# One store and one load a tile in a fused attention and gated MLP block, y and the result on GpSimd's queue, and the first half of w_in loaded early

## The chip, the cores and the metric

The kernel runs on one core of a Trainium2 chip. A core has five engines with an instruction stream each: TensorE (PE in the profile, with its weight loads as PEld), VectorE (DVE), ScalarE (ACT), GpSimd (POOL) and SyncE (SP), which only issues transfers. A transfer (DMA) is issued by an instruction on one of these streams, waits there for what it needs, and is then carried by the core's 16 DMA engines; "SPq", "ACTq" and "POOLq" are the issuing streams. The metric is the device time of the program in microseconds (us), lower is better; the time before is the median of three runs.

## The reference

One transformer block on x of 2048 tokens (S) by 640 (D), all in float32:

```python
h  = x + A_ref(layernorm(x), wqkv, wo)
h2 = h + B_ref(layernorm(h), w_in, w_sp, b_sp, w_out)
```

`A_ref` is attention with 32 heads of 20 values, causal, over a window of 256 tokens, followed by the projection with `wo`. `B_ref` is a gated MLP that mixes tokens:

```python
z = gelu(x @ w_in)                      # 2048 x 1728
z1, z2 = z[..., :864], layernorm(z[..., 864:])
g = w_sp @ z2 + b_sp[:, None]           # over tokens, 2048 x 2048
out = (z1 * g) @ w_out
```

## The kernel before

Tokens are cut into 16 tiles of 128. Every float32 product on TensorE is made of three products of a high and a low part (hi x hi, hi x lo, lo x hi), so each operand is first split: ScalarE or VectorE rounds the high part, VectorE subtracts it from the raw value for the low part. The two large products of the MLP use a scheme of seven block products instead of eight, whose block sums VectorE, ScalarE or GpSimd form beforehand.

The stages, in order of time. First layernorm, v, q and k. Then attention in 128 steps (`for s in range(NU + 2)`, L662), in which SP's order is the order in which the code is written; the sums of the softmax go through DRAM (`o_d`, then `r_d`, read back as `rs`). Then for each tile i `wo_tile(i)` (L1354): it scales o by the reciprocal sums (`norm_o`, L168), splits it (`split_o`, L173 to L177), multiplies it with wo (`proj_o`, L98), adds x (`load_x2` brings it, L144), and makes the layernorm of the result, `hn(i)`, in one of six buffers `hb`. `store_hn(i)` (L853) writes hn to DRAM. `z_pair` (L879) reads the rows of hn back with `load` (L896), turns them with a 32x32 block transpose on VectorE (L859), splits them and makes the first half of z (z1) with the first half of w_in; the blocks of that half are prepared by `win1_prep` (L779), a generator of which `wo_tile` takes three pieces a tile. `z2_pair` does the second half, `first_gate` and `second_gate` the products with w_sp, each over half of the tokens. In `second_gate(p)` (L1265) the gate is added up in `rows`, multiplied with z1 into y (`gated`, L1282), and y of two tiles is stored (`store_y`, L1210), loaded back with its blocks moved (`load_y`, L1215), turned (`turn_y`, L1220) and split (`split_y`, L139 and L140). `final` (L1244) multiplies it with w_out two pairs later, adds h (`load_h`, L1242) and stores the result (L1261). The last four tiles run behind the last step (L1412).

Both round trips through DRAM (hn, y) exist because VectorE transposes only within 32x32 blocks: the trip moves the blocks to other partitions. Before, hn's store is cut in four, one for each group of 32 tokens, and writes rows whose parts are already in block order; y's store is one transfer and its load is four:

```python
for a in range(4):
    nc.sync.dma_start(dst[a], hn(i)[32 * a:32 * a + 32].rearrange("j (b c) -> j b c", b=4))
```

Behind attention (`ms.close()`, L701) the order on each engine is not the order of the code: a planner orders every instruction by the code's order and by its own estimate of when its inputs are there. A `dict` named `later` (`at(n, f)`, L870) gives the step before which a piece of work is written. An engine executes its stream in order: an instruction that waits holds up all behind it.

w_in's first half has 5 row blocks of 128 x 864. Blocks 0 and 2 are loaded at step 126 of attention (L224) into `wraw`, blocks 1 and 3 into two of the `rows` buffers behind the third piece of `win1_prep` (L791), block 4 into `wraw` again behind the seventh (L793).

Of the kernel before, what the change touches and what calls it, by code (L numbers as in the profile page):

```python
# [15 lines left out]
P = 128  # L16
# [19 lines left out]
def block_kernel(ctx, tc, x, wqk, wv, wo, w_in, wsp, bsp, w_out, out):  # L36
# [19 lines left out]
    hn_d = dram.tile([NT, P, D], F32, name="hn_d")  # L56
# [49 lines left out]
    def open_early(pl):  # L106
        mem["m1"] = pl.tile([P, 6 * D + 6 * P], F32, name="m1")
        mem["xh"] = [pl.tile([P, D], F32, name=f"xh{i}") for i in range(4)]
        mem["inv"] = [pl.tile([P, P], F32, name=f"inv{i}") for i in range(2)]
        mem["wraw"] = pl.tile([P, 2, 2, HF], F32, name="wraw")  # L110
# [82 lines left out]
    def load_win1(b):  # L193
        nc.sync.dma_start(mem["wraw"][:, b], w_in[2 * b * P:(2 * b + 1) * P, :FH].rearrange("k (h c) -> k h c", h=2))

    def proj_early(s):
# [24 lines left out]
        if s == 125:  # L221
            split_o(1, True)
        if s == 126:
            for b in range(2):  # L224
                load_win1(b)
            tiles, mem["rs"], _ = load_o(2)
            tiles()
        if s == 127:
            for i in (2, 3):
                load_x2(i)  # L230
# [548 lines left out]
    def win1_prep(raw):  # L779
        seven, last = win1  # L780
        rest = [r.rearrange("p (h c) -> p h c", h=2) for r in rows[2:]]

# [4 lines left out]
        for n, f in enumerate(pieces(0, [raw[:, b] for b in range(2)], 1.0)):  # L787
            f()
            if n == 2:
                for b in range(2):  # L790
                    nc.sync.dma_start(rows[2 + b], w_in[(2 * b + 1) * P:(2 * b + 2) * P, :FH])  # L791
            yield
        nc.sync.dma_start(raw[:, 0], w_in[4 * P:, :FH].rearrange("k (h c) -> k h c", h=2))  # L793
        yield
        yield
        for f in pieces(1, rest, ones[:, 0:1]):
            f()
            yield
        yield
        for j in range(2):  # L800
            hi, lo = two(last[j])
            nc.scalar.activation(hi, raw[:, 0, j], AF.Copy, scale=ones[:, 1:2])
            minus(lo, raw[:, 0, j], hi.bitcast(F32))
        yield
# [13 lines left out]
    mem["xh"].append(ep.tile([P, D], F32, name="xh4"))  # L818
    mem["hb"] = [ep.tile([P, D], F32, name=f"hb{i}") for i in range(6)]
# [33 lines left out]
    def store_hn(i):  # L853
        dst = hn_d[i].rearrange("(b j) (a c) -> a j b c", b=4, a=4)
        for a in range(4):
            nc.sync.dma_start(dst[a], hn(i)[32 * a:32 * a + 32].rearrange("j (b c) -> j b c", b=4))
# [22 lines left out]
    def z_pair(q, i, j, w):  # L879
# [16 lines left out]
        def load():  # L896
            nc.sync.dma_start(ri, hn_d[i])
            nc.sync.dma_start(rj, hn_d[j])
# [550 lines left out]
```

## Time and profile before

| | |
|---|---|
| median of three runs | 1097.06 us (1095.64 to 1097.12) |
| the profiled execution's own time | 1099.3 us |
| its span, first to last instruction | 1097.6 us |
| mean granted clock of TensorE | 0.993 |
| HBM read and written | 129.00 MB and 72.86 MB |

The profile is of one execution. A row of a timeline gives start and length in us, engine, line, operation, output and inputs, and how often; in brackets stands the idle time of the engine before it and what ended it. A row of a source view gives min/median/max in ns, first and last start. A busy TensorE is not TensorE at its peak, but an idle one is lost time as long as nothing later absorbs it.

### The profile page before, as it was taken

To read this page: it belongs to the slowest core of one execution; us is meant where nothing else is said; L and a number is where in the kernel's file an instruction comes from. 1 tells how busy PE (TensorE), PEld (TensorE's weight loads), DVE (VectorE), ACT (ScalarE), POOL (GpSimd) and SP (SyncE) were. 2 spreads that over 40 slices of the span, in tenths; PEclk is the share of its full clock that TensorE was granted. 3 is DMA by queue.
4 is the path that set the end of the run, shared out by engine and by line. 5 is a ranking of instruction groups with operands and counts; after the bars stand their busy time and mean duration, and the time that the engine had idled before them with its cause. 6 is when DMAs were issued, how large, how long until landed. Compare 5 with 4: busy or idle time off the path is not lost.

```text
span 1097.6 us, 27487 instructions
## 1 busy us (share of the span) xinstructions
PE 1068.1 (97%) x10475; PEld 959.0 (87%) x10475; DVE 750.4 (68%) x2059; ACT 559.3 (51%) x1164; POOL 367.9 (34%) x526
## 2 busy tenths in 40 slices
PE   8999999999999999998999999999999999999998
PEld 7998877668888787698999999899999989989998
DVE  6541222879999999768867687767737895766553
ACT  4333443239999999747755567433426531222110
POOL 3114444457777777701000065265332000000000
PEclk9999999999999999999999999999999999999999
DMA  7212565565666664589855521456493587877554
GB/s 264 73 36 89 162 221 183 180 222 182 206 209 209 200 204 122 155 286 273 277 183 164 200 88 39 136 183 222 175 334 141 183 261 195 247 209 212 166 158 131
DMA packets 113077, 202.47 MB, mean 184 GB/s; under 512 B 13696, under 2 KB 74768, under 8 KB 109024
## 3 DMA queue, kind: packets, MB, share of 16 engines
q1 hardware_dynamic: 108304, 186.77, 53.8%
q0 software_dynamic: 2336, 8.70, 2.2%
q10 hardware_dynamic: 2304, 5.24, 1.3%
q8 instruction: 82, 1.34, 0.5%
q14 instruction: 51, 0.42, 0.1%
HBM read 129.00 MB, written 72.86 MB: 184 GB/s over the span
## 4 chain that ended last, share of the span: by engine, by line
PE 64%; DVE 11%; DMA 10%; issue 4%; POOL 4%; ACT 4%; SPq 2%; POOLq 0%; DVEq 0%; ACTq 0%
PE bank_a L1177 17%; PE bank_b L1235 6%; PE pv L437 6%; PE bank L343 5%; PE bank L409 5%; PE bank_a L929 4%; PE bank_b L929 3%; PE wo_ps L98 2%; PE qk L527 2%; PE qk L528 2%; PE qk L529 2%; DVE row L724 2%; ACT pt L412 2%; DVE zl L724 2%; PE bank_a L982 1%
## 5 line engine op out<-in xcount | busy, mean ns | idle before, releaser
L412 ACT ACTIVATE pt<-bank 128x384 f32<-128x384 f32 (+2 forms) x512 | 200.9, 497 | 10.5 <-PE bank L409 6.5
L1177 PE MATMUL bank_a<-zl,aw 128*128 128x432 f32 x759 | 168.1, 358 | 0.0
L355 DVE CUSTOM_DVE_ANT_0 junk<-bank,strip 128x288 bf16<-128x288 f32 x392 | 157.8, 454 | 3.3 <-PE bank L343 1.7
L730 ACT ACTIVATE aw<-fx 128x512 fp32r<-128x512 f32 (+3 forms) x147 | 85.1, 592 | 135.9 <-PE bank_a L1177 65.2
L1177 PEld LDWEIGHTS bank_a<-zl,aw 128*128 128x128 f32 x759 | 142.6, 188 | 6.0
L1177 PE MATMUL bank_a<-ze,aw 128*128 128x432 f32 x573 | 132.5, 359 | 4.1 <-DVE row L724 1.8
L437 PE MATMUL pv<-pt,v_sb 128*32 128x192 f32 (+3 forms) x1984 | 126.2, 322 | 2.9 <-POOL pt L414 1.1
L1177 PEld LDWEIGHTS bank_a<-ze,aw 128*128 128x128 f32 x573 | 106.1, 188 | 11.2 <-DVE row L724 2.9
L724 DVE TENSOR_TENSOR aw<-fx,aw 128x512 fp32r<-128x512 f32 (+3 forms) x146 | 100.1, 697 | 13.1 <-ACT aw L730 12.2
L409 PE MATMUL bank<-slot 123*32 123x288 bf16 (+5 forms) x1536 | 106.0, 280 | 1.6 <-ACT pt L412 0.7
L414 POOL TENSOR_SCALAR_AFFINE_SELECT pt<-pt 128x512 f32<-128x512 f32 x128 | 82.9, 648 | 44.5 <-ACT pt L412 43.4
L724 DVE TENSOR_TENSOR row<-bank_a,row 128x432 f32<-128x432 f32 x95 | 56.9, 602 | 58.0 <-PE bank_a L1177 40.9
L1235 PE MATMUL bank_b<-wout,y_sp 128*128 128x320 f32 (+1 forms) x588 | 92.1, 313 | 3.0 <-DVE y_sp L140 2.0
L982 PE MATMUL bank_a<-win,aw 128*128 128x432 f32 x480 | 95.0, 359 | 0.0
L982 PEld LDWEIGHTS bank_a<-win,aw 128*128 128x128 f32 x480 | 90.4, 188 | 3.8
L1235 PEld LDWEIGHTS bank_b<-wout,y_sp 128*128 128x128 f32 (+1 forms) x588 | 89.6, 191 | 4.1 <-DVE y_sp L140 2.4
L343 PE MATMUL bank<-slot 120*32 120x288 bf16 (+2 forms) x1264 | 89.1, 283 | 1.5 <-DVE mcol L355 1.0
L543 DVE TENSOR_TENSOR rest<-qk,sg 128x512 f32<-128x512 f32 x40 | 27.7, 692 | 86.9 <-ACT sg L541 86.9
L417 POOL TENSOR_SCALAR_AFFINE_SELECT pt<-pt 128x512 f32<-128x512 f32 x112 | 74.5, 665 | 0.0
L546 POOL TENSOR_TENSOR sg<-rest,sg 128x512 bf16<-128x512 f32 x40 | 46.6, 1166 | 70.1 <-ACT sg L545 65.8
L409 PEld LDWEIGHTS <-slot 123*32 123x32 bf16 x1536 | 52.6, 96 | 16.7 <-issue 5.7
L437 PEld LDWEIGHTS pv<-pt,v_sb 128*32 128x32 f32 x1984 | 59.1, 110 | 8.5 <-POOL pt L417 3.0
(198 smaller groups left out, 2178.6 us busy)
## 6 DMA issues: line engine op xcount, KB each, us to landing
fx<-wsp_in SPq DMA_DIRECT2D x30, 512.0 KB
slot<-qk_d SPq DMA_DIRECT2D x72, 200.0 KB
qk_d<-sg SPq DMA_DIRECT2D x32, 384.0 KB
slot<-qk_d SPq DMA_DIRECT2D x72, 160.0 KB
fx<-hn_d SPq DMA_DIRECT2D x32, 320.0 KB
o_d<-ot SPq DMA_DIRECT2D x64, 128.0 KB
z_d<-row SPq DMA_DIRECT2D x18, 432.0 KB
y_d<-z SPq DMA_DIRECT2D x16, 448.0 KB
```

The costliest lines, as they stand in the source:

```text
L343: nc.tensor.matmul(ps[32 * j:32 * j + 32, :n], part(st, half, 120, 0, hh, q0, 32), part(st, half, 120, 1, hh, lo + skip * j, n), start=Tru ...
L355: nc.vector.tensor_tensor_reduce(out=junk[:, :n], in0=ps[:, :n], in1=keep, scale=1.0, scalar=NEG, op0=OP.add, op1=OP.max, accum_out=m_cols ...
L409: nc.tensor.matmul(ps[32 * i:32 * i + 32, b:e], part(st, half, 123, 1, hh, k0, 32), part(st, half, 123, 0, hh, kb * P + b, e - b), start=T ...
L412: nc.scalar.activation(pt[:, hh, :n], ps[:, :n], AF.Exp, scale=SCALE)
L414: nc.gpsimd.affine_select(out=pt[:, :, :P], in_=pt[:, :, :P], pattern=[[0, 4], [1, P]], base=0, channel_multiplier=-1, compare_op=OP.is_ge ...
L437: nc.tensor.matmul(ps[32 * hh:32 * hh + 32, a - 512 * c:b - 512 * c], v_sb[:, kb, v0:v0 + 32], pt[:, hh, a - kb * P:b - kb * P], start=fir ...
L724: (eng or nc.vector).tensor_tensor(out=out, in0=a, in1=b, op=op)
L730: nc.scalar.activation(out, a, AF.Copy)
L929: nc.tensor.matmul(ps, a[x], b[:, y], start=start and m + x + y == 0, stop=stop and m == n - 1 and x == 1, skip_group_check=True)
L982: nc.tensor.matmul(b[0][:, :HF], a[t][:, x, kk], win2[0][:, y, kk, h * HF:(h + 1) * HF], start=kk + x + y == 0, stop=kk == KD - 1 and x == 1)
L1177: nc.tensor.matmul(ps, w[m][x][:, k], zc[k][m][:, y], start=start and k + x + y == 0, stop=stop and k == 3 and x == 1, skip_group_check=True)
L1235: nc.tensor.matmul(ps[j][:, :HD], y[:w, a, k, :], e1["wout"][:w, b, k, j * HD:(j + 1) * HD], start=(k == 0 and a + b == 0), stop=(k == KF ...
```

## The change

hn is stored in one transfer, as four planes of 160 columns (`hn_d` is now `[NT, 4, P, D // 4]`), and read back with four consecutive tokens in one row of 640 (`hn_rows`). The tokens of a tile therefore come out of the transpose in another order: position 32a + j holds token 4j + a. z, z1, z2 and g keep that order, and w_sp and b_sp are permuted to it on the host. y's load takes the same form, in one transfer, and orders the tokens once more; h is loaded and the result is stored through a view (`twice_turned`) that has the same order on the DRAM side.

y's stores and loads and the result's stores of the first 12 of 16 tiles are issued on GpSimd (`queue(n)`); those of the last four stay on SP. h's loads stay on SP.

All five blocks of w_in's first half have a tile of their own in `wraw` and are loaded at attention's steps 114 to 122, one at every second step. `wo_tile` takes three pieces of `win1_prep` for the first two tiles and two for the others. The fifth buffer of x (`xh`) is opened with the others, the load of x's tile 4 moves to step 127, and hn has five buffers in place of six.

```diff
-    hn_d = dram.tile([NT, P, D], F32, name="hn_d")
+    hn_d = dram.tile([NT, 4, P, D // 4], F32, name="hn_d")
...
-        mem["wraw"] = pl.tile([P, 2, 2, HF], F32, name="wraw")
+        mem["wraw"] = [pl.tile([P, 2, HF], F32, name=f"wraw{i}") for i in range(KD)]
...
-        nc.sync.dma_start(mem["wraw"][:, b], w_in[2 * b * P:(2 * b + 1) * P, :FH].rearrange("k (h c) -> k h c", h=2))
+        nc.sync.dma_start(mem["wraw"][b], w_in[b * P:(b + 1) * P, :FH].rearrange("k (h c) -> k h c", h=2))
...
+        if 114 <= s < 124 and s % 2 == 0:
+            load_win1((0, 2, 1, 3, 4)[(s - 114) // 2])
         if s == 126:
-            for b in range(2):
-                load_win1(b)
             tiles, mem["rs"], _ = load_o(2)
             tiles()
         if s == 127:
-            for i in (2, 3):
+            for i in (2, 3, 4):
                 load_x2(i)
             mem["rs"]()
...
-        for n, f in enumerate(pieces(0, [raw[:, b] for b in range(2)], 1.0)):
-            f()
-            if n == 2:
-                for b in range(2):
-                    nc.sync.dma_start(rows[2 + b], w_in[(2 * b + 1) * P:(2 * b + 2) * P, :FH])
-            yield
-        nc.sync.dma_start(raw[:, 0], w_in[4 * P:, :FH].rearrange("k (h c) -> k h c", h=2))
-        yield
-        yield
-        for f in pieces(1, rest, ones[:, 0:1]):
-            f()
-            yield
-        yield
+        for k in range(2):
+            for f in pieces(k, [raw[k], raw[k + 2]], ones[:, 0:1] if k else 1.0):
+                f()
+                yield
...
-    mem["hb"] = [ep.tile([P, D], F32, name=f"hb{i}") for i in range(6)]
+    mem["hb"] = [ep.tile([P, D], F32, name=f"hb{i}") for i in range(5)]
...
     def store_hn(i):
-        dst = hn_d[i].rearrange("(b j) (a c) -> a j b c", b=4, a=4)
-        for a in range(4):
-            nc.sync.dma_start(dst[a], hn(i)[32 * a:32 * a + 32].rearrange("j (b c) -> j b c", b=4))
+        nc.sync.dma_start(hn_d[i].rearrange("b p c -> p b c"), hn(i).rearrange("p (b c) -> p b c", b=4))
+
+    def hn_rows(i):
+        return hn_d[i].rearrange("b (j a) c -> (b j) (a c)", a=4)
...
+    def queue(n):
+        return nc.gpsimd if n < NT - 4 else nc.sync
+
     def store_y(n):
-        nc.sync.dma_start(y_d[n].rearrange("b p c -> p b c"),
+        queue(n).dma_start(y_d[n].rearrange("b p c -> p b c"),
                           e1["z1"][n % 2].rearrange("p (b c) -> p b c", b=4))

     def load_y(n):
-        for b in range(4):
-            nc.sync.dma_start(e1["yt"][n % 2][32 * b:32 * b + 32].rearrange("j (a c) -> j a c", a=4),
-                              y_d[n, b].rearrange("(a j) c -> j a c", a=4))
+        queue(n).dma_start(e1["yt"][n % 2], y_d[n].rearrange("b (j a) c -> (b j) (a c)", a=4))
...
+    def twice_turned(d):
+        return d.rearrange("(b a) c -> a b c", a=16)
+
     def load_h(n):
-        nc.sync.dma_start(e1["h"][n % 2], h_d[tile_of(n)])
+        nc.sync.dma_start(e1["h"][n % 2], twice_turned(h_d[tile_of(n)]))
...
-            nc.sync.dma_start(out[tile_of(n) * P:(tile_of(n) + 1) * P, c], ht[:, c])
+            queue(n).dma_start(twice_turned(out[tile_of(n) * P:(tile_of(n) + 1) * P, c]), ht[:, c])
...
-        for n in (4,) if i == 0 else (i + 4,) if i + 4 < NT else ():
-            load_x2(n)
+        if 0 < i < NT - 4:
+            load_x2(i + 4)
...
-        for _ in range(3):
+        for _ in range(3 if i < 2 else 2):
             next(w1, None)
...
-    wsp = np.asarray(B_w_sp).reshape(NT, P, NT, P).transpose(0, 3, 2, 1)
-    bsp = np.asarray(B_b_sp).reshape(NT, P).T
+    order = np.arange(P).reshape(32, 4).T.reshape(P)
+    wsp = np.asarray(B_w_sp).reshape(NT, P, NT, P)[:, order][..., order].transpose(0, 3, 2, 1)
+    bsp = np.asarray(B_b_sp).reshape(NT, P)[:, order].T
```

More of the change, by code (lines that the diff above doesn't have):

```diff
@@ L107, in open_early @@
         mem["m1"] = pl.tile([P, 6 * D + 6 * P], F32, name="m1")
-        mem["xh"] = [pl.tile([P, D], F32, name=f"xh{i}") for i in range(4)]
+        mem["xh"] = [pl.tile([P, D], F32, name=f"xh{i}") for i in range(5)]
         mem["inv"] = [pl.tile([P, P], F32, name=f"inv{i}") for i in range(2)]
-        mem["wraw"] = pl.tile([P, 2, 2, HF], F32, name="wraw")
+        mem["wraw"] = [pl.tile([P, 2, HF], F32, name=f"wraw{i}") for i in range(KD)]
     def view(flat, lo, *shape):
@@ L780, in win1_prep @@
         seven, last = win1
-        rest = [r.rearrange("p (h c) -> p h c", h=2) for r in rows[2:]]
         def pieces(k, blocks, one):
@@ L786, in win1_prep @@
         yield
-        for n, f in enumerate(pieces(0, [raw[:, b] for b in range(2)], 1.0)):
-            f()
-            if n == 2:
-                for b in range(2):
-                    nc.sync.dma_start(rows[2 + b], w_in[(2 * b + 1) * P:(2 * b + 2) * P, :FH])
-            yield
-        nc.sync.dma_start(raw[:, 0], w_in[4 * P:, :FH].rearrange("k (h c) -> k h c", h=2))
-        yield
-        yield
-        for f in pieces(1, rest, ones[:, 0:1]):
-            f()
-            yield
-        yield
+        for k in range(2):
+            for f in pieces(k, [raw[k], raw[k + 2]], ones[:, 0:1] if k else 1.0):
+                f()
+                yield
         for j in range(2):
             hi, lo = two(last[j])
-            nc.scalar.activation(hi, raw[:, 0, j], AF.Copy, scale=ones[:, 1:2])
-            minus(lo, raw[:, 0, j], hi.bitcast(F32))
-        yield
+            nc.scalar.activation(hi, raw[4][:, j], AF.Copy, scale=ones[:, 1:2])
+            minus(lo, raw[4][:, j], hi.bitcast(F32))
+            yield
     def win2_prep(raw):
@@ L817, in block_kernel @@
     ep = pool(early_stack, "early2")
-    mem["xh"].append(ep.tile([P, D], F32, name="xh4"))
-    mem["hb"] = [ep.tile([P, D], F32, name=f"hb{i}") for i in range(6)]
+    mem["hb"] = [ep.tile([P, D], F32, name=f"hb{i}") for i in range(5)]
     zc_stack, win_stack = (ctx.enter_context(ExitStack()) for _ in range(2))
@@ L896, in load @@
         def load():
-            nc.sync.dma_start(ri, hn_d[i])
-            nc.sync.dma_start(rj, hn_d[j])
+            nc.sync.dma_start(ri, hn_rows(i))
+            nc.sync.dma_start(rj, hn_rows(j))
         a11, a12, a21, a22 = (turned(r, k, k + 2) for r in (ri, rj) for k in (0, 2))
@@ L990, in z2_pair @@
             soon = q == 13
-            at(m - (5 if soon else 12 if q == 8 else 6), lambda t=t, tile_t=tile_t: nc.sync.dma_start(r[t], hn_d[tile_t]))
+            at(m - (5 if soon else 12 if q == 8 else 6), lambda t=t, tile_t=tile_t: nc.sync.dma_start(r[t], hn_rows(tile_t)))
             at(m - (1 if soon else 3), lambda t=t: prep(t, True, None))
```

## The prediction

> **What bounds the kernel now.** I read the page first, then the table of stages, then TensorE's timeline wherever a stage shows it idle, and then the queue (SP) and VectorE (DVE) at those places.
>
> ```profile
> span 1097.6 us, 27487 instructions
> PE 1068.1 (97%) x10475; PEld 959.0 (87%) x10475; DVE 750.4 (68%) x2059; ACT 559.3 (51%) x1164; POOL 367.9 (34%) x526
> ```
>
> TensorE (PE) is idle for 1097.6 - 1068.1 = 29.5 us of the span. Only idle time of PE, and time in which its clock is lowered, can be won by a change that touches transfers alone. The stages show where that is; the columns are stage, length, busy us of PE, weight load, DVE, ACT, POOL, granted clock, DMA share and GB/s.
>
> ```profile
> 428.00:440.00 12.00, 11.11 (x289) 8.23 (x285) 10.52 (x32) 11.47 (x34) 10.21 (x18) 1.00 0.35 105
> 440.00:465.00 25.00, 22.48 (x431) 15.20 (x424) 17.67 (x22) 18.80 (x52) 18.96 (x25) 1.00 0.48 143
> 465.00:525.00 60.00, 54.02 (x322) 52.30 (x323) 47.91 (x115) 35.30 (x66) 6.61 (x8) 0.91 0.89 280
> 525.00:630.00 105.00, 105.00 (x581) 101.74 (x580) 75.49 (x165) 65.31 (x118) 6.80 (x9) 1.00 0.64 204
> 880.00:970.00 90.00, 85.53 (x485) 81.94 (x486) 63.72 (x104) 21.00 (x32) 0.00 (x0) 1.00 0.81 238
> 970.00:1071.00 101.00, 101.00 (x585) 98.74 (x584) 61.18 (x96) 19.03 (x26) 0.00 (x0) 0.98 0.61 176
> ```
>
> The change works in two stages with losses. In 465 to 525 (attention over, first output projections and z products) PE idles 5.98 us, its clock is 0.91, and the DMA engines are 89% busy. In 880 to 970 (start of the second gates) it idles 4.47 us. From 525 to 630, where most of hn's stores lie, and from 970 to 1071, PE is never idle: there the change can win nothing.
>
> **The gaps of 465 to 525 on PE** (in brackets the idle time before the row, and what ended it):
>
> ```profile
> 480.94 0.85 PE L98 MATMUL wo_ps<-xb,xb 128*128 128x320 f32 x4 [2.02 <-DVE xb L177]
> 514.10 1.01 PE L929 MATMUL bank_b<-zl,aw 128*128 128x432 f32 x3 [1.24 <-ACT tmp L730]
> 517.83 1.45 PE L929 MATMUL bank_b<-zl,aw 128*128 128x432 f32 x3 [2.72 <-DVE aw L724]
> ```
>
> The same stretch in tens of microseconds (columns as above):
>
> ```profile
> 480.00:490.00 10.00, 9.06 (x51) 9.06 (x52) 8.01 (x19) 5.39 (x10) 0.85 (x1) 0.83 0.88 287
> 490.00:500.00 10.00, 10.00 (x70) 10.00 (x69) 9.31 (x24) 6.11 (x11) 2.64 (x3) 1.00 0.93 307
> 500.00:510.00 10.00, 10.00 (x67) 9.91 (x66) 10.00 (x24) 6.87 (x15) 0.66 (x1) 1.00 0.95 282
> 510.00:520.00 10.00, 6.04 (x25) 4.94 (x24) 7.01 (x18) 7.30 (x14) 1.91 (x2) 0.81 0.86 254
> 520.00:530.00 10.00, 10.00 (x53) 9.64 (x53) 8.08 (x22) 6.98 (x13) 0.55 (x1) 0.85 0.88 274
> ```
>
> The gaps are 2.02 + 1.24 + 2.72 = 5.98 us. A clock of 0.83, 0.81 and 0.85 over 10 us costs 1.7, 1.9 and 1.5 us; at half clock that is 3.4 us behind the first gap, and 3.8 + 3.0 us around the last two. If the second spell is unbroken it began at 516.2, so that 1.6 us of it lie inside the gap that ends at 517.83 and cost nothing more (0.8 us taken off): 1.7 + 2.6 = 4.3 us. The stage loses 5.98 + 4.3 = 10.3 us.
>
> The Trainium skill (TensorE: Matmul & The Clock Gate, section "Part 1: The HAM clock gate (the "warmup" mystery)") has the clock halve after an idle window of about 3.4 us; by that rule a gap of 2.02 us would cost nothing more and the stage could give back 5.98 us only. The trace disagrees: 0.83 behind a gap of 2.02 us.
>
> **What is late there.** The queue before the first gap, and before the last:
>
> ```profile
> 445.47 3.17 SPq L152 DMA_DIRECT2D m<-o_d  x5
> 462.58 1.06 SPq L194 DMA_DIRECT2D wraw<-w_in_in  x2
> 463.68 4.46 SPq L152 DMA_DIRECT2D m<-o_d  x5
> 468.24 0.58 SPq L392 DMA_DIRECT2D r_d<-inv  x1
> 471.38 0.52 SPq L158 DMA_DIRECT2D m<-r_d  x1
> 474.97 1.56 DVE L168 TENSOR_TENSOR m<-m 128x640 f32<-128x640 f32 x2 [4.57 <-DMA m<-r_d]
> 498.00 1.77 SPq L856 DMA_DIRECT2D hn_d<-hb  x4
> 500.35 2.48 SPq L856 DMA_DIRECT2D hn_d<-hb  x4
> 503.40 2.57 SPq L856 DMA_DIRECT2D hn_d<-hb  x4
> 509.48 0.60 SPq L158 DMA_DIRECT2D m<-r_d  x1
> 514.75 1.56 DVE L168 TENSOR_TENSOR m<-m 128x640 f32<-128x640 f32 x2 [2.99 <-DMA m<-r_d]
> ```
>
> DVE waits twice for reciprocal row sums (m<-r_d). The store that they are read back from goes out at 468.24 only after two loads of w_in and five slow ones of o_d; the later load goes out at 509.48 after three groups of hn stores. Everything behind these waits on DVE, the split that PE needs included (L177, L724), comes late.
>
> **The change, part by part.** *hn's store as one issue.* The layout in DRAM still has runs of 160 values (640 B), so packets and bytes stay; 64 issues become 16. Their price is that of y's store, also one issue of 128 x 4 runs:
>
> ```profile
> L856 SPq DMA_DIRECT2D hn_d<-hb x64: 302/432/1056, 476.9 to 586.1; - x64
> L1210 SPq DMA_DIRECT2D y_d<-z x16: 370/377/434, 875.8 to 1072.7; - x16
> ```
>
> The queue wins 64 x 0.432 - 16 x 0.377 = 21.6 us, but on the path only the three groups count: 1.77 + 2.48 + 2.57 - 3 x 0.377 = 5.7 us, against a DVE wait of 2.99. The read side keeps whole rows; the new token order costs nothing on the chip, since w_sp and b_sp are permuted on the host and h and the result keep one run a row in the DRAM side's new order.
>
> *w_in's five loads moved* to steps 114 to 122 of 128, that is to about 428 to 446 (an estimate: step 126 issued its two loads at 462.58, and a step takes some 2 to 3 us). They pass attention's stores and o_d's first loads on the queue (five issues, some 0.5 us each, where the queue is not full). 5 x 432 KB at 280 GB/s is 7.9 us of transfers that leave the stage behind 462.58 (two there; the code has two more behind the third of w_in's pieces and one behind the seventh) and enter stages at 105 to 143 GB/s, so I put them at nothing there; uncovered, one load's 1.6 us would delay attention's last store. On the path they give 1.06 us of issue, and the five loads behind them go from 4.46 back to 3.17 us if the engines are less full: 2.35 us, against a gap of 2.02. x2's fifth load, now before L158, adds one issue of about 0.5 us that the wait before 471.38 hides.
>
> *Sum of this stage.* If both chains close, 2.02 + 1.7 and 2.72 + 2.6 = 9.0 us are won; the gap of 1.24 waits for ACT and stays. Against it: DVE has no slack in 490 to 510 (9.31 and 10.00 of 10), so what comes earlier still meets its backlog, and 5 buffers for hn instead of 6 make a tile wait for the store five before (stores at 498.00, 500.35 and 503.40 are 2.7 us apart, so that one is 13 us old; y's store, below, has landed by 3.4 us: nothing). Ends 0 and 10.3; I take two thirds of 9.0, **6 us**.
>
> *y and the result on GpSimd's queue.* POOL has 0.00 busy from 880 on, so nothing of its own is delayed. SP loses 12 of 16 tiles' stores, loads and results. What counts is the round trip of y: at 983.61 the store is issued, at 987.04 the load, at 994.77 it has landed.
>
> ```profile
> 983.61 0.37 SPq L1210 DMA_DIRECT2D y_d<-z  x1
> 987.04 1.80 SPq L1215 DMA_DIRECT2D yt<-y_d  x4
> 994.77 1.11 DVE L1220 STREAM_TRANSPOSE yt<-yt 128x896 f32<-128x896 f32 x1 [5.33 <-DMA yt<-y_d]
> 996.58 1.07 DVE L140 TENSOR_TENSOR y_sp<-yt,y_sp 128x896 fp32r<-128x896 f32 x1
> 998.52 0.74 PE L1235 MATMUL bank_b<-wout,y_sp 128*128 128x320 f32 x4
> zp_d<-side_parts POOLq DMA_DIRECT2D x7, 432.0 KB, 3.5
> wp_d<-side_parts POOLq DMA_DIRECT2D x7, 512.0 KB, 7.0
> side_raw<-wsp_in POOLq DMA_DIRECT2D x4, 256.0 KB, 5.9
> side_raw<-z_d POOLq DMA_DIRECT2D x2, 432.0 KB, 4.3
> ```
>
> The trip now takes 11.2 us. Behind the waiting transpose (L1220) stands the split of the tile that PE wants next (L140, done at 997.65; PE takes it at 998.52): the slack is 0.87 us, so a trip of up to 12.0 us is free. Nothing of y runs on POOL yet; the nearest rows are its stores of 432 and 512 KB (median 3.5 and 7.0) and loads (4.3 and 5.9): from 7.8 to 12.9 us. Nearest in size are 3.5 + 4.3 = 7.8, so no loss in the steady stage; in 880 to 970 a shorter trip and a freer SP can give from 0 to the 4.47 us of idle. I take **1 us**.
>
> The Trainium skill (DMA: Bandwidth & Descriptors, section "Issuing engines are not separate DMA queues") speaks against this part: another issuer saves only the sequencer's time, 1.80 us a tile here, where SP is not the bound. By that rule this part gives 0 and the total is 6.
>
> *Order.* Behind attention the order on every engine comes from the planner, whose estimates change with the transfers; the trace of before cannot show the new order. I bound it by one stretch such as 880 to 970 more or fewer, 4.5 us either way, and take 0.
>
> Sum: -6 - 1 = -7 us. The profiled execution takes 1099.3 us (the span and 1.7 around it), 2.2 above the median of 1097.06; 7 less is 1092.3 for it and **1090** for the median.
>
> **Rivals.** (1) *DVE keeps the time* (18%). If the backlog of 490 to 510 sets the first z product, only the first gap closes: 2.02 us, some clock behind it, -2.5 us: 1094.5. For it speaks 10.00 of 10; against it that the backlog itself starts behind the wait of 4.57.
>
> (2) *Everything closes* (12%). All of 10.3, the 4.47 of 880 to 970, and the clock of 0.98 over the 101 us behind it (2.0): 16.8 us, 1080. Against it speaks the gap that waits for ACT.
>
> (3) *Slower: y's trip on GpSimd's queue becomes the wait* (17%). The place is L1220 ahead of L140, once a pair, in the six pairs whose tiles go by POOL. It costs what the trip takes over 12.0 us. The longest landings on that queue are
>
> ```profile
> DMA to landing us min/median/max: 3.0/3.5/7.5
> DMA to landing us min/median/max: 3.2/4.8/7.5
> ```
>
> for the 432 KB stores and for the loads: 15.0 us, 3.0 over, 18 us in six pairs, and with the 6 won early +12: 1109. It decides from a trip of 13.0 us on (6 x 1.0 cancels the 6). For it: the engines are 81% busy from 880 to 970, and 61% behind. Against it: the medians.
>
> (4) *It doesn't do what it says* (8%). The three hn groups and w_in leave the path, but the planner fills the place with other loads, and L158 goes out as late as before: 0, 1097.
>
> **How the numbers follow.** The forecast has 45%, its own range 1086 to 1094. Changes under 0.2% (2.2 us) can't be told from none here. Faster: 0.43 of the forecast, all of (2), half of (1): 0.64. Same: 0.02 + 0.09 + 0.05 of (4) = 0.16. Slower: 0.17 + 0.03 = 0.20. The range leaves out half of (2) and the far half of (3): 1082 to 1104.
>
> **What would show it.** Right: 16 issues on L856 at about 0.4 us; w_in's loads between 428 and 450; L168 waiting under 1 us for m<-r_d; no gap over 1.3 us between 475 and 525 and a clock of 1.00 there; L1220 waiting no longer than 5 us with trips under 12. Wrong: L168 waiting as before (step of the queue), PE idle in 465 to 525 named after DVE with no DMA behind it (rival 1), gaps on L1235 behind L1220 after 970 (rival 3), a new gap in 440 to 465 (w_in's loads collide with attention's end).

## The result: slower, and the profile after

The changed kernel takes **1106.85 us** (median of 6, 1103.42 to 1109.56), beside 1096.35 us (1093.19 to 1099.20) for the kernel before on the same chip: a ratio of 1.0086, 95% interval 1.0067 to 1.0105. The forecast was 1090, its range 1082 to 1104. The profiled execution took 1109.56 us with a span of 1107.9, 10.3 more than the span before.

The page of the kernel after, its head; then three rows of its table of stages (columns as in the prediction):

```profile
span 1107.9 us, 27379 instructions
PE 1069.8 (97%) x10475; PEld 960.0 (87%) x10475; DVE 751.1 (68%) x2059; ACT 558.5 (50%) x1164; POOL 391.2 (35%) x562
```

```profile
465.00:525.00 60.00, 51.00 (x320) 48.91 (x318) 44.12 (x95) 27.93 (x53) 4.97 (x6) 0.89 0.78 247
880.00:970.00 90.00, 85.63 (x477) 82.62 (x476) 69.64 (x116) 24.32 (x37) 11.70 (x18) 0.98 0.70 227
970.00:1071.00 101.00, 99.92 (x589) 97.38 (x588) 61.14 (x95) 19.65 (x27) 10.18 (x17) 1.00 0.61 195
```

PE is idle for 1107.9 - 1069.8 = 38.1 us instead of 29.5. Of that, 465 to 525 now holds 9.00 us (5.98 before), with a lower clock (0.89 for 0.91), and 970 to 1071, which had none, holds 1.08. The idle time of 880 to 970, of which I hoped to win some, is still there: 4.37 us for 4.47. Its transfers now take a smaller share of the DMA engines (0.70 for 0.81), and that buys nothing.

The gaps on PE's timeline after the change, in attention's last steps and the first output projections, and then in the second gates:

```profile
486.50 0.90 PE L98 MATMUL wo_ps<-xb,xb 128*128 128x320 f32 x2 [5.65 <-ACT xb L176]
488.88 0.90 PE L98 MATMUL wo_ps<-xb 128*128 128x320 f32 x2 [0.94 <-ACT xb L176]
492.72 1.43 PE L98 MATMUL wo_ps<-xb,xb 128*128 128x320 f32 x4 [2.41 <-DVE xb L177]
526.24 0.66 PE L918 MATMUL bank_a<-zl,aw 128*128 128x432 f32 x2 [1.14 <-ACT aw L730]
529.37 0.88 PE L918 MATMUL bank_a<-zl,aw 128*128 128x432 f32 x2 [2.08 <-DVE aw L724]
...
905.57 1.44 PE L1225 MATMUL bank_b<-wout,y_sp 128*128 128x320 f32 x4 [3.21 <-ACT y_sp L139]
1008.82 1.44 PE L1225 MATMUL bank_b<-wout,y_sp 128*128 128x320 f32 x8 [1.08 <-DVE y_sp L140]
```

The first gap has grown from 2.02 to 5.65 us and comes 5.6 us later. The two gaps on L1225, where the product of the result waits for y's split, had forerunners in the kernel before (1.02 us at 923.30 and 1.99 at 969.67, by its timeline); now they stand elsewhere, and the first is larger and comes with the first pair of tiles.

For the runs below I use two lengths in each profiled execution, both between first and last starts of products: **head**, from the first output projection (wo) to the first gate product, and **gates**, from the first to the last gate product. They come from one execution of each kernel. In the ten kernels that load w_in late the head is between 225.2 and 229.4 us, so a difference of less than some 4 us is not read.

| kernel | median us | ratio to before (95%) | head | gates |
|---|---|---|---|---|
| before | 1096 to 1097 | 1 | 225.5 | 385.4 |
| after | 1106.85 | 1.0086 (1.0067 to 1.0105) | 234.0 | 384.1 |

The head alone got 8.5 us longer. It also begins 2.3 us later (462.1 us for 459.8); in the other kernels it begins between 457.7 and 462.1, and I did not follow that up. What follows splits the loss.

### The profile page after: what moved, and what is told of

Same layout as the page of the kernel before. It is cut to its first block, busy times and chain, and to the rows that moved or that the text cites. A ratio compares the mean times of both kernels' runs of the same rounds, so it can differ in the third digit from the quotient of the medians.

```text
span 1107.9 us, 27379 instructions
## 1 busy us (share of the span) xinstructions
PE 1069.8 (97%) x10475; PEld 960.0 (87%) x10475; DVE 751.1 (68%) x2059; ACT 558.5 (50%) x1164; POOL 391.2 (35%) x562
## 4 chain that ended last, share of the span: by engine, by line
PE 69%; DVE 9%; DMA 9%; issue 5%; POOL 3%; ACT 3%; SPq 2%; ACTq 0%; POOLq 0%; DVEq 0%
PE bank_a L1166 19%; PE bank_b L1225 8%; PE pv L437 6%; PE bank L343 5%; PE bank L409 5%; PE wo_ps L98 5%; PE bank_a L918 4%; PE bank_b L918 3%; PE qk L527 2%; PE qk L528 2%; PE qk L529 2%; DMA fx<-wsp_in 2%; DVE zl L724 2%; DMA fx<-hn_d 2%; DVE row L724 1%
## 5 line engine op out<-in xcount | busy, mean ns | idle before, releaser
L730 ACT ACTIVATE aw<-fx 128x512 fp32r<-128x512 f32 (+3 forms) x147 | 84.8, 591 | 131.3 <-PE bank_a L1166 81.6
L409 PE MATMUL bank<-slot 123*32 123x288 bf16 (+6 forms) x1536 | 105.7, 280 | 2.6 <-issue 1.7
L1225 PE MATMUL bank_b<-wout,y_sp 128*128 128x320 f32 (+1 forms) x588 | 90.9, 311 | 4.3 <-ACT y_sp L139 3.2
L1225 PEld LDWEIGHTS bank_b<-wout,y_sp 128*128 128x128 f32 (+1 forms) x588 | 88.4, 189 | 5.4 <-ACT y_sp L139 3.6
```

The costliest lines, as they stand in the source:

```text
L409: nc.tensor.matmul(ps[32 * i:32 * i + 32, b:e], part(st, half, 123, 1, hh, k0, 32), part(st, half, 123, 0, hh, kb * P + b, e - b), start=T ...
L730: nc.scalar.activation(out, a, AF.Copy)
L1225: nc.tensor.matmul(ps[j][:, :HD], y[:w, a, k, :], e1["wout"][:w, b, k, j * HD:(j + 1) * HD], start=(k == 0 and a + b == 0), stop=(k == KF ...
```

## The experiments

### Each move undone by itself

One kernel puts only w_in's loads back to where the kernel before has them; one puts only y and the result back on SP; one adds the early loads, with the buffers and the pace of the pieces that go with them, to the kernel before; and one issues the early loads all together, at step 112. The edits to the changed kernel, in this order (the third is the w_in part of the change's diff, in the kernel before):

```diff
-        if 114 <= s < 124 and s % 2 == 0:
-            load_win1((0, 2, 1, 3, 4)[(s - 114) // 2])
         if s == 126:
+            for b in (0, 2):
+                load_win1(b)
...
+                if k == 0 and n == 2:
+                    load_win1(1)
+                    load_win1(3)
+                if k == 0 and n == 6:
+                    load_win1(4)
```

```diff
     def queue(n):
-        return nc.gpsimd if n < NT - 4 else nc.sync
+        return nc.sync
```

```diff
-        if 114 <= s < 124 and s % 2 == 0:
-            load_win1((0, 2, 1, 3, 4)[(s - 114) // 2])
+        if s == 112:
+            for b in (0, 2, 1, 3, 4):
+                load_win1(b)
```

> The changed kernel with w_in's five loads put back where the kernel before has them (blocks 0 and 2 at step 126, 1 and 3 behind the third piece, 4 behind the seventh); all else as changed. Theory A (w_in's loads, issued from 441 to 465 us, stand in the queue and in the engines ahead of the o_d stores and of the round trip of the softmax sums, and cost the 8.3 us by which the stretch from the first output projection to the last z product grew, 170.7 to 179.0): that stretch back to 171 or less, time 1092 to 1099. Rival B (the new order behind attention, which follows from the single hn store and the new buffers, costs it): stretch 177 to 181, time 1104 to 1108.

> The changed kernel with y's transfers and the result's stores of all 16 tiles on SP. Theory A: the gates took 384.1 us in the changed kernel and 385.4 before, so GpSimd's queue is worth about 1 us at most: time 1105 to 1109, gates 383 to 387. Rival C (the slower round trip on GpSimd's queue costs the 10 us): 1096 to 1099, gates under 380.

> The kernel before with w_in's five loads early, with their five tiles, x's fifth buffer and load, hn's five buffers and the pacing of the pieces; hn's four stores, y's four loads and SP as the only queue stay. Theory A: the stretch from the first output projection to the last z product 177 to 182 (170.7 before), time 1102 to 1108. Rival B: 170 to 172, time 1095 to 1098.

> The changed kernel with all five w_in loads at step 112, so that they are issued from about 436 to 441 us, ahead of the first store of the sums' round trip. Theory A: most of the loss goes, since 5 x 432 KB are through by about 450: stretch 170 to 174, time 1095 to 1101. If it is the bytes anywhere in attention's last steps that cost: 177 to 181, time 1104 to 1108.

| kernel | median us | ratio to before (95%) | head | gates |
|---|---|---|---|---|
| w_in late | 1101.10 | 1.0030 (1.0012 to 1.0048) | 227.0 | 385.8 |
| y on SP | 1099.87 | 1.0030 (1.0011 to 1.0049) | 233.9 | 379.8 |
| before, w_in early | 1100.43 | 1.0026 (1.0008 to 1.0044) | 230.0 | 381.2 |
| w_in at step 112 | 1104.93 | 1.0068 (1.0044 to 1.0092) | 228.5 | 387.5 |

Either move, taken back, wins 0.0056 of the 0.0086, each in its own place. The early loads cost in the head (234.0 to 227.0), GpSimd's queue in the gates (384.1 to 379.8). My expectations were off: w_in late came out between its two ranges, and for y on SP I had expected 1105 to 1109. Added to the kernel before, the early loads cost there too: 4.5 us of head, 0.26% in all. In that kernel the gates are 4.2 us shorter than before though nothing of theirs was touched; I did not follow up why. Five loads at once, ahead of the round trips of the row sums, give back most of the head (228.5 for 234.0), but the gates are the longest of all (387.5, not followed up), and the time can't be told from the changed kernel's.

### Both undone: what the layout is worth, and whether the losses add

```diff
     def queue(n):
-        return nc.gpsimd if n < NT - 4 else nc.sync
+        return nc.sync
```

This edit is made to the kernel with w_in late; what stays of the change is the order of the tokens, one store of hn and one load of y a tile, w_in in five tiles, five buffers of hn, the early load of x's tile 4, and the pace of w_in's pieces. I call it the layout.

> The change with both of its moves undone: the single stores of hn, the single loads of y and the new order of the tokens stay; w_in's loads go out where the kernel before has them, and y and the result go by SP. If the losses of the two moves add (1106.85 to 1101.1 without the early loads, 1106.85 to 1099.87 without GpSimd's queue), the rest is 1106.85 - 5.8 - 7.0 = 1094, 0.997 of the kernel before. Rival: the two losses are one and the same (a shift of the order that either move causes), then taking away both gives no more than taking away one: 1100, 1.003. By the steps of my prediction the single stores alone are worth up to 5.7 us: 1092, with hn's issues at 16 x 0.4 us.

Measured: 1094.83 us, 0.9978 (0.9960 to 0.9995), head 227.8, gates 379.3. **The losses add**: from 0.9978, each move alone costs 0.0052 (to 1.0030), and both together 0.0108, 11.8 us of 1096.5. This version is faster than before by 0.2%, the whole of what the layout brings. It does not bring it in the head. PE's two large gaps there, and a piece of the chain of waits in the same kernel:

```profile
483.53 0.90 PE L98 MATMUL wo_ps<-xb 128*128 128x320 f32 x2 [3.03 <-DVE zl L724]
516.34 2.14 PE L923 MATMUL bank_b<-zl,aw 128*128 128x432 f32 x5 [4.98 <-DVE mvc L1371]
```

```profile
503.94 6.14 DMA hn_d<-hb
```

Of DVE's two waits for the row sums the second (2.99 us) is gone: after the first, no wait that is put down to m<-r_d is longer than 0.32 us. The first is still there, at the same time and as long (4.41 us at 475.21, in the profile put down to a store of o_d, for 4.57 at 474.97). And the large gaps of PE are 3.03 and 4.98 us where there were 2.02 and 3.96 (1.24 + 2.72). The first now waits for a piece of w_in (zl) that DVE does ahead of the split of o, the second for DVE, which has waited for the rows of hn: by the chain their store alone takes 6.14 us.

### The single store and the single load, each cut up again

In the version of 1094.83 us, hn's store and y's load were cut into four issues of 32 rows each; the layout stays.

```diff
-        nc.sync.dma_start(hn_d[i].rearrange("b p c -> p b c"), hn(i).rearrange("p (b c) -> p b c", b=4))
+        for a in range(4):
+            r = slice(32 * a, 32 * a + 32)
+            nc.sync.dma_start(hn_d[i][:, r].rearrange("b p c -> p b c"), hn(i)[r].rearrange("p (b c) -> p b c", b=4))
```

```diff
-        queue(n).dma_start(e1["yt"][n % 2], y_d[n].rearrange("b (j a) c -> (b j) (a c)", a=4))
+        for b in range(4):
+            queue(n).dma_start(e1["yt"][n % 2][32 * b:32 * b + 32], y_d[n, b].rearrange("(j a) c -> j (a c)", a=4))
```

> The version that took 1094.83 us (single stores and loads, w_in late, all of y on SP), but with hn's store cut again into four issues of 32 rows; the layout stays. My prediction put the single store at 5.7 us of SP's time ahead of the row sums, most of it won: then this takes 1098 to 1100. Rival (the store's issues were not what the end waits for: with w_in late the stage from the first product of wo to the last z1 product took 173.1 us with the single store and 170.7 in the kernel before): no difference, 1094 to 1096, with 64 issues of about 0.4 us on the store's line.

> The same version with y's load cut again into four issues a tile; the layout stays. Theory (what the layout wins lies in the stage of the gates, 379.2 us from first to last against 385.4 before, because one load a tile frees SP and lands earlier): the stage goes back to 383 to 386 and the time to 1098 to 1100, with idle PE of 2 to 4.5 us in 880 to 970. Rival (it came from the planner's order, which the new estimates of time changed, not from the issues): 1094 to 1096, PE idle about 1.2 there.

| kernel | median us | ratio to before (95%) | head | gates |
|---|---|---|---|---|
| hn in four stores | 1096.58 | 0.9998 (0.9982 to 1.0014) | 229.4 | 379.4 |
| y in four loads | 1100.01 | 1.0015 (0.9996 to 1.0035) | 226.0 | 382.4 |

For **hn** the result lies between the two expectations, and the intervals with one store and with four overlap (0.9960 to 0.9995 and 0.9982 to 1.0014): a gain of some 2 us can't be excluded, the 5.7 of the prediction can. For **y** they just part: 0.9978 against 1.0015, about 4 us, and it shows in the trace. The second gates in the version with one load (first row) and with four (second), each kernel's stage of 880 to 970; and PE's gaps with four loads:

```profile
880.00:970.00 90.00, 88.82 (x511) 86.23 (x510) 70.25 (x114) 22.96 (x34) 0.00 (x0) 1.00 0.78 260
```

```profile
880.00:970.00 90.00, 85.75 (x490) 82.54 (x489) 65.55 (x107) 22.07 (x33) 0.00 (x0) 1.00 0.82 245
```

```profile
893.13 0.85 PE L1171 MATMUL bank_a<-ze,aw 128*128 128x432 f32 x3 [1.49 <-DVE row L724]
969.69 5.86 PE L1231 MATMUL bank_b<-wout,y_sp 128*128 128x320 f32 x38 [1.60 <-DVE y_sp L140]
```

PE is idle for 1.18 us with one load and for 4.25 with four, about as before (4.47). So the load of y is what the layout wins, and it wins it in the stage where the prediction had put "from 0 to the 4.47 us of idle". The gates agree over all kernels: 378.0 to 379.8 us in the six with y's store on SP and one load, 381.2 to 385.4 in the three with four loads on SP. How much of it is the landing and how much the planner's new order, which came with it, is not taken apart.

### Why w_in's early loads cost: their place in SP's line

In the changed kernel the five loads leave SP at these times:

```profile
441.37 0.42 SPq L194 DMA_DIRECT2D wraw<-w_in_in  x1
442.60 0.45 SPq L194 DMA_DIRECT2D wraw<-w_in_in  x1
454.30 1.07 SPq L194 DMA_DIRECT2D wraw<-w_in_in  x2
464.52 0.58 SPq L194 DMA_DIRECT2D wraw<-w_in_in  x1
```

The chain of waits of the changed kernel through these loads:

```profile
454.95 4.82 DMA wraw<-w_in_in
459.83 4.11 DMA r_d<-inv
465.67 6.04 DMA o_d<-ot
478.87 5.36 DMA m<-r_d
```

Attention's tail is a chain through one queue: store o, load its row sums (inv), store the reciprocals (r_d), load them back (m). Each link waits for the landing of the one before. A load of 432 KB that stands between two links can delay all that follow. By the chain the first store of r_d is released by the landing of a w_in load, 4.82 us, of whose data it needs none; SP's own rows show the queue issuing loads of o_d until 459.52, so that this link may only be how the profile infers releasers. The store of o behind the fifth load lands in 6.04 us, where the chain of the kernel before has

```profile
459.19 2.78 DMA o_d<-ot
```

for it. What DVE then meets, on its timeline in the changed kernel:

```profile
484.44 1.56 DVE L168 TENSOR_TENSOR m<-m 128x640 f32<-128x640 f32 x2 [7.10 <-DMA m<-r_d]
```

7.10 us in place of 4.57. To tell the place in the line from the bytes in flight, the same five loads were issued on ACT's queue: first in the changed kernel, then in the one with y on SP.

```diff
-        nc.sync.dma_start(mem["wraw"][b], w_in[b * P:(b + 1) * P, :FH].rearrange("k (h c) -> k h c", h=2))
+        nc.scalar.dma_start(mem["wraw"][b], w_in[b * P:(b + 1) * P, :FH].rearrange("k (h c) -> k h c", h=2))
```

> The changed kernel with w_in's five early loads issued on ACT's queue instead of SP's, at the same steps: the same 2.1 MB at about the same time, but nothing on SP stands in line behind them. Theory (the place in SP's line costs: the loads stand between attention's last stores and the read-back of the row sums): the time falls by most of the 5.8 us that the early loads cost, 1101 to 1103, and r_d<-inv goes out earlier than 459.83, 475.63, 483.96 and 490.86. Rival (the bytes in flight cost: o_d's store and the read-back are slow because w_in fills the engines): as the changed kernel, 1105 to 1108, with o_d<-ot again landing 6 us after its issue.

> w_in's five loads early as in the change, but issued on ACT's queue, and all of y and the result on SP: beside the version of 1094.83 it differs only in the loads of w_in, beside the one of 1099.87 only in their queue. Theory (their place in SP's line is the cost): ratio to the kernel before 0.997 to 1.000, the stage from the first wo product to the last z1 product 171 to 174 us, r_d<-inv issued within 2 us of 455, 468, 477 and 483. Rival (their bytes are the cost, on any queue): ratio 1.003, the stage 177 to 180.

| kernel | median us | ratio to before (95%) | head | gates |
|---|---|---|---|---|
| after, w_in on ACT's queue | 1103.62 | 1.0064 (1.0039 to 1.0089) | 227.4 | 385.3 |
| the same, y on SP | 1098.22 | 1.0017 (0.9999 to 1.0034) | 227.6 | 378.9 |

By the time alone the two queues can't be told apart: ACT's wins back 0.0022 and 0.0013, within the intervals, where late loads win back 0.0056 and 0.0052. The head does tell: 227.4 and 227.6, as with w_in late (227.0 and 227.8), not 234. (The profiled executions with 234.0 and 233.9 were 2.7 and 4.2 us slower than the medians of their kernels, so that a typical head may be somewhat shorter.) The stores of r_d in this stretch, in the kernel before, in the changed kernel, and with the loads on ACT's queue and y on SP (count, shortest/median/longest issue in ns, first and last start):

```profile
L392 SPq DMA_DIRECT2D r_d<-inv x4: 562/582/602, 455.0 to 482.1; - x4
```

```profile
L392 SPq DMA_DIRECT2D r_d<-inv x4: 564/570/578, 459.8 to 490.9; - x4
```

```profile
L392 SPq DMA_DIRECT2D r_d<-inv x4: 569/576/603, 455.4 to 482.6; - x4
```

The last goes out at 482.6, as before, not at 490.9. So in the head it was the place in SP's line and not the bytes. The whole time does not come back: 1.0017 against 0.9978 with w_in late, and these intervals do not overlap. A part is seen in ACT's rows of that run, where ACT stands still around its fifth issue (at 451.80), in attention:

```profile
452.25 3.94 ACT L412 ACTIVATE pt<-bank 128x384 f32<-128x384 f32 x10 [2.19 <-DMA m<-o_d]
```

That is 2.2 us, and PE waits with it (2.04 us at 452.80). The profiled execution (1096.63 us) is about as quick as that of the version with w_in late (1096.34); the rest of the difference of the medians stays unexplained.

The same run asks what w_in in SP's line had cost before. With the loads early and off that line, the store of r_d that went out at 468.24 goes out at 467.57, DVE scales o at 475.55 (474.97 before), and PE's gaps at this place are

```profile
480.66 0.56 PE L98 MATMUL wo_ps<-xb 128*128 128x320 f32 x2 [0.59 <-ACT xb L176]
482.97 0.85 PE L98 MATMUL wo_ps<-xb,xb 128*128 128x320 f32 x4 [1.46 <-DVE xb L177]
```

2.05 us together, for 2.02 before. The two loads at 462.58 were not what that gap waited for.

### Why GpSimd's queue costs: y's store

The changed kernel's transfers of y on that queue (KB each, median us from issue to landing):

```profile
y_d<-z POOLq DMA_DIRECT2D x12, 448.0 KB, 7.6
yt<-y_d POOLq DMA_DIRECT2D x12, 448.0 KB, 5.7
```

The seven stores of zp_d on the same queue, 432 KB each in whole rows, land in 3.4 there. y's trip is 7.6 + 5.7 = 13.3 us by these medians. Two kernels, both with w_in late, tell which part of the move costs: one has only the result's stores back on SP, the other only y's stores.

```diff
-            queue(n).dma_start(twice_turned(out[tile_of(n) * P:(tile_of(n) + 1) * P, c]), ht[:, c])
+            nc.sync.dma_start(twice_turned(out[tile_of(n) * P:(tile_of(n) + 1) * P, c]), ht[:, c])
```

```diff
-        queue(n).dma_start(y_d[n].rearrange("b p c -> p b c"),
+        nc.sync.dma_start(y_d[n].rearrange("b p c -> p b c"),
```

> The change with w_in's loads late and the result's stores back on SP; y's stores and loads stay on GpSimd's queue. Theory (y's own trip is the cost: 7.6 us to land a store and 5.7 a load, 13.3 against my limit of 12.0): the loss stays, 1100 to 1102, with gaps ahead of the product of the result at the first pair and near 1000. Rival (the result's stores, each waiting for DVE, hold up y's loads that stand behind them on the same queue): the loss goes, 1094 to 1096, and no gap there.

> The change with w_in's loads late and y's stores back on SP; y's loads and the result's stores stay on GpSimd's queue. Theory (the trip is the cost, and in it the store with its 512 runs of 896 B, 7.6 us against some 3.4 by SP): the trip falls to about 9 us, under the 12.0, and the loss goes: 1094 to 1096. Rival (the result's stores ahead of y's loads in the one queue): it stays, 1099 to 1102. Second rival (transfers of two queues share the engines, so that w_sp's loads on SP land late, 8 to 10 us, whatever the direction): it falls by half, 1097 to 1098.

| kernel | median us | ratio to before (95%) | head | gates |
|---|---|---|---|---|
| result's stores on SP | 1100.69 | 1.0037 (1.0017 to 1.0057) | 226.0 | 382.8 |
| y's stores on SP | 1094.63 | 0.9975 (0.9960 to 0.9991) | 227.4 | 378.0 |

**The whole loss is y's store.** With it on SP, y's loads and the result's stores can stay on GpSimd's queue at no cost (0.9975 against 0.9978 with all on SP), and at no gain.

With only the result's stores on SP the gap at the first pair came as expected, and the one near 1000 did not.

The loss is not there because the trip exceeds a limit of 12.0 us. With w_in late, the first tile of the first pair is stored at 877.24 and turned at 889.03, 11.8 us, and PE has a gap of 3.02 us for it (rows of five engines in order of time; fx<-wsp_in is the load of w_sp):

```profile
877.24 0.82 POOL L1207 DMA_DIRECT2D y_d<-z  x1 [17.79 <-DVE onew L1321]
884.07 1.82 SPq L1099 DMA_DIRECT2D fx<-wsp_in  x2
889.03 1.11 DVE L1215 STREAM_TRANSPOSE yt<-yt 128x896 f32<-128x896 f32 x1 [0.74 <-DMA yt<-y_d]
894.64 0.63 ACT L730 ACTIVATE aw<-fx 128x512 fp32r<-128x512 f32 x1 [4.83 <-DMA fx<-wsp_in]
895.18 0.93 ACT L139 ACTIVATE y_sp<-yt 128x896 fp32r<-128x896 f32 x1
896.16 1.16 PE L1230 MATMUL bank_b<-wout,y_sp 128*128 128x320 f32 x4 [3.02 <-ACT y_sp L139]
```

y's split (L139) stands on ACT behind a split of w_sp (L730) that waits 4.83 us for its load, and PE waits with it. In the version of 1094.83 us the two have changed places, and the wait for w_sp holds up nothing that PE wants at once:

```profile
890.97 0.94 ACT L139 ACTIVATE y_sp<-yt 128x896 fp32r<-128x896 f32 x1
893.60 1.16 ACT L730 ACTIVATE aw<-fx 128x512 fp32r<-128x512 f32 x2 [1.70 <-DMA fx<-wsp_in]
```

All six kernels with y's store on GpSimd's queue have this order and a gap of 2.4 to 4.4 us ahead of the first product of y, named after ACT's split; none of those with it on SP has such a gap there. But the order alone does not make it. The kernel before has the same order:

```profile
884.30 0.85 SPq L1105 DMA_DIRECT2D fx<-wsp_in  x2
891.31 0.63 ACT L730 ACTIVATE aw<-fx 128x512 fp32r<-128x512 f32 x1 [2.04 <-DMA fx<-wsp_in]
891.85 0.94 ACT L139 ACTIVATE y_sp<-yt 128x896 fp32r<-128x896 f32 x1
```

and so have the kernel before with w_in early and the one with four loads of y, all three without a gap ahead of that product. In these three the split of w_sp starts 7.0 to 7.1 us after the two loads begin to go out, in the six with y's store on GpSimd's queue 8.5 to 10.6 us after. So two things come together there: y's split stands behind w_sp's, and w_sp's load, on SP's queue, comes later. That is the mechanism of the second rival in the run with y's stores on SP (w_sp late while another queue moves y), but for the stores alone: with y's loads and the result's stores on GpSimd's queue, and y's stores on SP, the split starts 8.0 us after, and nothing is lost. At the fifth pair DVE waits 5.6 to 8.2 us for w_sp ahead of the turn of y in five of the six, and four of them have a gap of 1.1 to 1.9 us there. What in y's store delays w_sp's load, the rows do not say, and neither the order nor the lateness was changed alone.

### How slow the store is, and of what

In the version of 1094.83 us, y's store goes by GpSimd's queue in whole rows (128 runs of 3584 B), and the load, on SP, takes the short runs:

```diff
-        queue(n).dma_start(y_d[n].rearrange("b p c -> p b c"),
-                          e1["z1"][n % 2].rearrange("p (b c) -> p b c", b=4))
+        (nc.gpsimd if n < NT - 4 else nc.sync).dma_start(y_d[n], e1["z1"][n % 2])
...
+        for b in range(4):
+            nc.sync.dma_start(e1["yt"][n % 2][32 * b:32 * b + 32].rearrange("j (a c) -> j a c", a=4),
+                              y_d[n].rearrange("(j a) (b c) -> b j a c", a=4, b=4)[b])
```

> The same version with y's store on GpSimd's queue in whole rows, 128 runs of 3584 B in place of 512 of 896 B; the load, on SP, then takes the short runs, in four issues of 128 runs. Theory (GpSimd's store is slow by its number of runs: 7.6 us for 512 of y, 3.4 for 128 of zp_d of nearly the same bytes): the store lands in 3.5 to 5 us, and the time is that of the version with four loads on SP (so within 2 us of the kernel of the four loads, 1094 to 1100). Rival (it is slow by what else SP moves at that time): it lands in 7 to 8 us as before, and the time is 1100 to 1103.

In the other kernel y's stores are unchanged but go by ACT's queue:

```diff
-        queue(n).dma_start(y_d[n].rearrange("b p c -> p b c"),
+        (nc.scalar if n < NT - 4 else nc.sync).dma_start(y_d[n].rearrange("b p c -> p b c"),
```

> The version that took 1094.83 us, with y's stores of twelve tiles on ACT's queue; all else of y and the result stays on SP. Same 512 runs of 896 B, a second queue beside SP's, but not GpSimd's. Theory (GpSimd's queue itself makes the store slow, 7.6 us): the store is as quick as by SP and the time stays at 1094 to 1097, ratio to the kernel before 0.996 to 1.000, PE without a gap of 2 us near 896. Rival (any second queue shares the engines with SP's loads of w_sp, and both land late): ratio 1.003 to 1.005, a gap of 2.4 to 3.2 us near 896.

The first takes 1101.52 us, 1.0028 (1.0007 to 1.0049), gates 385.4; its store lands in

```profile
y_d<-z POOLq DMA_DIRECT2D x12, 448.0 KB, 5.5
```

between the two expectations, with a time in the rival's range: fewer runs take 2.1 us off the 7.6, and the 5.5 are still above zp_d's 3.4. The gap ahead of y's product stays (4.36 us at 898.54, after ACT's split). The second takes 1098.61 us, 1.0014 (0.9990 to 1.0037), between the expectations as well; PE has the gap that the rival named:

```profile
896.48 0.85 PE L1230 MATMUL bank_b<-wout,y_sp 128*128 128x320 f32 x4 [2.68 <-ACT y_sp L139]
```

ACT's split of y stands there behind a wait of 7.27 us for w_out, another order once more. How long the store takes on each queue can be read at the fifth pair, where SP's next load of z waits for it, first in the version of 1094.83 us, then with y's store on ACT's queue:

```profile
980.13 0.38 SPq L1207 DMA_DIRECT2D y_d<-z  x1
983.15 0.32 SPq L1283 DMA_DIRECT2D z<-z_d  x1
```

```profile
984.44 0.43 ACTq L1207 DMA_DIRECT2D y_d<-z  x1
989.66 0.32 SPq L1283 DMA_DIRECT2D z<-z_d  x1
```

3.0 us from SP and 5.2 from ACT. From GpSimd, with only the result's stores on SP, y's load goes out 5.2 us after its store at this pair. So the store is slower from either second queue, and not from GpSimd's alone. What ACT's queue costs in time stays open.

### What keeps the head from winning

In the version of 1094.83 us, w_in's pieces were handed to DVE two a tile for the first two tiles and three from then on.

```diff
-        for _ in range(3 if i < 2 else 2):
+        for _ in range(2 if i < 2 else 3):
```

> The version that took 1094.83 us, with w_in's splits handed out two a tile for the first two tiles and three from then on, where it has three and then two. It asks what keeps the stage of wo from winning what the single store of hn frees: there PE waits 3.03 us at 483.53 for a piece of w_in that DVE does ahead of the split of o (zl, L724), and 4.98 us at 516.34 for hn's own trip. Theory (the pieces of w_in take the place of the wait for the row sums): the gap at 483 falls under 2.5 us and the time to 1092 to 1094. Rival (DVE has as much to do either way, and the later gap takes what the first gives up): the gaps at 483 and 516 still sum to 7 to 9 us, time 1094 to 1097.

Measured: 1093.54 us, 0.9988 (0.9964 to 1.0012), head 226.1, gates 378.3. PE's gaps:

```profile
484.23 0.90 PE L98 MATMUL wo_ps<-xb 128*128 128x320 f32 x2 [3.32 <-DVE zl L724]
514.28 1.43 PE L923 MATMUL bank_b<-zl,aw 128*128 128x432 f32 x6 [1.92 <-DVE mvc L1371]
```

Neither expectation holds: the first gap did not move (3.32 for 3.03), the second fell from 4.98 to 1.92. By its ratio this can't be told from the version it started from. The version with y's stores alone on SP and w_in late (0.9975) and the one of 1094.83 us (0.9978) are the only two whose interval lies below the kernel before.

## Why the prediction was wrong

*w_in's five loads: "I put them at nothing there".* This step failed: the loads cost 0.0052 to 0.0056 of ratio in the changed kernel, some 6 us, and 6 to 7 us of head (0.0026 when added to the kernel before). Two things were off. The place: "about 428 to 446 (an estimate ... a step takes some 2 to 3 us)"; they left SP between 441.37 and 464.52. Written at the same steps, but issued on ACT's queue, they went out between 436.54 and 451.80: on SP they had waited behind what stands before them in the line. And the price: "uncovered, one load's 1.6 us would delay attention's last store" counts bytes over bandwidth once, while the chain of round trips passes the loads several times; one of its links alone grew from 2.78 to 6.04 us. The gain of 2.35 us that I listed was not there either: with the loads early and out of SP's line the store of r_d goes out 0.67 us earlier, and PE's gaps stay at 2.05 us. I had asked what the loads are covered by, and not what stands behind them on their queue. The gap did not come where I listed it (from 440 to 465 PE idles 2.01 us, 2.52 before) but where the chain ends, at 481 to 493.

*"L168 waiting under 1 us for m<-r_d".* In the changed kernel the wait is 7.10 us, because of the loads. Without them the second of the two waits goes, as the step has it, the first stays at 4.41 us, and the gain does not come.

*hn's store as one issue: "on the path only the three groups count ... 5.7 us", and "6 us" for the stage.* The price of an issue was right: in the changed kernel the 16 issues on L842 take 0.376 us in the median. The term of the sum was 0 to about 2 us, by one store against four. With the later row sums out of the way, the head has other last arrivals: a piece of w_in on DVE, and hn's own trip. The prediction had named DVE's backlog as rival (1) and taken two thirds regardless.

*y's single load.* It was not a term of its own; I priced it inside "I take 1 us", out of 0 to 4.47. It is worth 0.0037 of ratio, 4 us, and this is all that the change can be shown to win.

*y on GpSimd's queue.* "So no loss in the steady stage" failed: 0.0052 to 0.0056, 6 us. I took the nearest size, 3.5 + 4.3 = 7.8, from stores in whole rows; y's store has four runs a row, and landed in 7.6 us against 3.4 for those. And I asked only whether y would be late, not what its store would do to the loads that SP moves at the same time: w_sp's came later, and ACT's split of y stood behind it. The Trainium skill's rule that I cited against this part (DMA: Bandwidth & Descriptors, section "Issuing engines are not separate DMA queues") has another issuer save only the sequencer's time; by it the move is worth nothing. Here it cost 6 us, so that the runs agree that there is nothing to win, but not that it is free.

*Rival (3)* had the sign, and the 13.3 us of the medians lie above its point of 13.0. Its mechanism failed: it expected the trip to cost what it takes over 12.0 us, in six pairs, 3 us each. The gaps are at the first pair and in some kernels at the fifth; the one at the first comes with a trip of 11.8 us, and y's split stands behind w_sp's.

*"The trace of before cannot show the new order ... and take 0".* Its bound, 4.5 us either way, was honest; the value was not 0. The gap of 3.21 us at 905.57 and that of 1.08 at 1008.82 lie within it.

The sum of what the runs give, in ratio: -0.0022 for the layout, +0.0052 for the early loads, +0.0052 for GpSimd's queue, together +0.0082, against +0.0086 measured.

## What to carry to other kernels

Before a load is put earlier, look at what stands behind it on the same queue: a chain of small round trips can pay for every large transfer that is put between its links. Before a transfer is moved to another queue, ask what the old queue moves at that time: here a load on SP came later, and the split that PE wanted stood behind it. Look in the trace for the instruction that PE waits for, and for what it now stands behind. Cutting four transfers to one pays only where the transfer's landing is the last to arrive: here y's load, and not hn's store.

## What the runs showed of the hardware

- On GpSimd's queue a store of 448 KB in 512 runs of 896 B landed in 7.6 us (median), one of the same size in 128 runs of 3584 B in 5.5, and one of 432 KB in whole rows, earlier in the kernel, in 3.4.
- At the fifth pair the store of 448 KB in 512 runs took 3.0 us from SP's queue and 5.2 from ACT's, until the load that waits for it went out; 5.2 from GpSimd's, until y's load went out.
- A load of w_sp on SP's queue, of 512 KB, was split 7.0 to 7.1 us after it and its neighbour began to go out in three kernels with y's store on SP, and 8.5 to 10.6 us in the six with y's store on GpSimd's queue.
- A store of 128 KB (o_d) landed in 2.78 us before, and in 6.04 behind a load of 432 KB issued just ahead of it on the same queue.
- PE's clock was lowered behind a gap of 3.03 us in the version of 1094.83 us, to a mean of 0.66 from 480 to 490:

```profile
480.00:490.00 10.00, 6.97 (x32) 6.71 (x31) 9.69 (x20) 3.09 (x6) 0.00 (x0) 0.66 0.89 260
```
